# Attention, expert layer and cosine layer on one core: scores kept out of the output bank, loads and 64-bit conversions put in another order

## The chip, the cores and the metric

One of the eight cores of a Trainium2 chip runs the whole program. The metric is the time of one execution on the device, in microseconds (us); where several executions are told, the median stands for them.

## The reference

Three layers follow each other. Shapes: q, k, v are (4, 8, 576, 64); there are 2304 tokens of width 512.

```python
scores = scale * (q @ k.T)                       # per batch and head
mask   = (rel >= 0) & (rel < 128)                # rel = row - column
scores = where(mask, scores - slope[h] * abs(rel), -1e9)
attn   = softmax(scores);  x = (attn @ v) as (2304, 512)

P = exp(x @ w_gate - max)                        # (2304, 8)
8 times:  P /= rowsum(P);  P /= colsum(P);  P *= N / E
x2 = sum over 8 experts e of  P[:, e] * (relu(x @ w1[e]) @ w2[e])      # F = 1024

h = x2 @ w_in;  out = (h * cos(h)) @ w_out       # d_ff = 2048
```

`w_in` and `w_out` arrive as 64-bit floats, so the kernel sees each of their numbers as two 32-bit words and makes 32-bit floats of them itself.

## The kernel before, in words

**Engines and queues.** TensorE (PE) multiplies, VectorE (DVE), ScalarE (ACT) and GpSimd (POOL) work elementwise, and nearly every DMA is issued by SyncE (SP). The program's order of instructions is written out by hand: the order in which the Python emits them is the order on each engine, and an engine whose next instruction waits holds all that stand behind it. Tiles are tracked whole: an instruction that writes a tile waits for the earlier readers of that tile, also where it writes another part of it.

**Attention** goes head pair by head pair: `pi` = 0 to 15 (4 batches of 4 head pairs), five groups `u` of 128 query rows each (the last has 64), 80 groups in all. One turn `i` of the main loop (line 790) takes the pair of groups 2i and 2i+1 and does, in this order: scores of pair i (`emit_qk`), exponentials of pair i-1 (`emit_exp`, ACT), bias and row maximum of pair i (`emit_max`, DVE, L547), `gates`, the product with v of pair i-4 (`emit_AV`), transposes of the next head pair's q and k (`heads`, which calls `emit_T`), the copy of a finished head pair into `xr` (`emit_x`), transposes of the probabilities of pair i-3 (`emit_PT`), the scaling by the row sums of pair i-1 (`emit_norm`, POOL, L586), and two calls of `side`.

`emit_T(pi, piece)` turns a quarter of a head pair's q and k round: pieces 0 and 1 are the first and second part of q, 2 and 3 those of k. T(1,3) below means head pair 1, piece 3. The copies out of PSUM are made by DVE (qT, qL, the first part of kT) and ACT (the second part of kT, L511).

**PSUM in attention.** `ps_s` holds two banks for scores, `ps_t` three for transposes, `ps_g` one that gates and the pieces 0 and 2 share, and `xbank` is one tile of two banks in which the product with v is summed and in whose end the pieces 1 and 3 are put. The scores of pair 1 and pair 3 are put in the front of `xbank` and in a bank of `ps_t` (L525).

**Loads of q, k and v.** Each of the three has two buffers. At u = 1 and u = 3 of head pair `pi`, `heads` issues q and k of `pi + 2`; v of `pi + 2` is issued when `pi` is finished. Each is three DMAs on SP (lines 462 and 468).

**Gates.** 384 tokens make a half block, of which four become ready within attention. `gates` first transposes the last half's logits (`gate_block2`, a DVE copy at L381) and then, in the same turn, starts the next half (`gate_block`, an ACT copy); both use the one bank of `ps_g`. Two halves are ready at once only after the second batch.

**64-bit conversion.** `convert_f64` (L255) is a generator of ten steps; its caller takes one step at a time. Its tile `f` (called `raw`) has one buffer, so the next load (`load_f64`, L245 or L251, 512 KB in one or two DMAs) waits on SP until the words have been read. Before: DVE takes the exponent (L260, step 1), ACT scales it (L264, step 2), DVE joins sign and exponent (L267, step 4), masks the mantissa (L271, step 5), adds the low word (L275, step 6) and multiplies (L279, step 7); the next load is in step 8 and the store of the result (L287) in step 10. `side` takes two steps a turn, for four conversions between n = 8 and n = 47. The other 28 run in the expert layer's second and third token block (about 670 to 1420 us).

**Expert layer, token blocks 1 and 2.** Each step (32 a block) makes seven products in the order m = 5, 1, 4, 2, 3, 6, 7 (L966); after each comes one *couple* with a half of a second-layer product (`s_step`, L1105). A couple takes its 12 matmuls in about 2.08 us. Every second couple SP loads 512 KB of second-layer weights into one of four slots of `wbX` (L1133), for use three pairs of couples later; first-layer weights (`waX`, L115) are loaded almost two steps ahead. After the couple of m = 5, 1, 4, 2 and 7 there are two slots, after 3 and 6 one; each slot takes one step of the conversion. A conversion that starts with a step of the layer thus has its steps 5 and 6 after m = 4 and its steps 7 and 8 after m = 2. A step has seven couples, so in every other step the load into `wbX` comes with the couple of m = 2, and in the others with those of m = 4 and m = 3.

Of the kernel before, what the change touches and what calls it, by code (L numbers as in the profile page):

```python
# [18 lines left out]
P = 128  # L19
# [10 lines left out]
def tile_attention_moe_cos_ffn(ctx, tc, q, k, v, w_gate, w1, w2, w_in, w_out, out):  # L30
# [41 lines left out]
    with tc.manual_schedule():  # L72
# [164 lines left out]
        def load_f64(c):  # L237
            if c >= 4 * NU2:
                return
            s, x = divmod(c, 4)  # L240
            raw = u_pool.tile([P, 512, 2], I32, tag="u0", name=f"f64_{c}")
            if x < 2:
                for y in range(2):
                    kc = 2 * x + y
                    nc.sync.dma_start(  # L245
                        out=raw[:, y * FU:(y + 1) * FU, :].rearrange("p n t -> p (n t)"),
                        in_=w_in[kc * P:(kc + 1) * P, 2 * s * FU:2 * (s + 1) * FU],
                    )
            else:
                r0 = s * FU + (x - 2) * P  # L250
                nc.sync.dma_start(out=raw.rearrange("p n t -> p (n t)"), in_=w_out[r0:r0 + P, :])  # L251
            f64_t[c] = raw

        def convert_f64(c):
            raw = f64_t.pop(c)  # L255
            lo, hi = raw[:, :, 0], raw[:, :, 1]
            a = u_pool.tile([P, 512], I32, tag="u1", name=f"fa{c}")
            b = u_pool.tile([P, 512], I32, tag="u2", name=f"fb{c}")
            w = b.bitcast(F32)
            nc.vector.tensor_scalar(  # L260
                out=a, in0=hi, scalar1=20, scalar2=0x7FF, op0=ALU.logical_shift_right, op1=ALU.bitwise_and
            )
            yield
            nc.scalar.activation(out=a, in_=a, func=AF.Relu, scale=2.0 ** 23, bias=ebias)  # L264
            yield
            yield
            nc.vector.scalar_tensor_tensor(  # L267
                out=a, in0=hi, scalar=-2147483648, in1=a, op0=ALU.bitwise_and, op1=ALU.bitwise_or
            )
            yield  # L270
            nc.vector.tensor_scalar(  # L271
                out=b, in0=hi, scalar1=0xFFFFF, scalar2=0x100000, op0=ALU.bitwise_and, op1=ALU.bitwise_or
            )
            yield
            nc.vector.scalar_tensor_tensor(  # L275
                out=w, in0=lo.bitcast(U32), scalar=2.0 ** -32, in1=b, op0=ALU.mult, op1=ALU.add
            )
            yield
            nc.vector.scalar_tensor_tensor(  # L279
                out=w, in0=w, scalar=2.0 ** -20, in1=a.bitcast(F32), op0=ALU.mult, op1=ALU.mult  # L280
            )
            yield
            load_f64(c + 1)
            yield
            yield
            w32[c] = dram.tile([P, 512], F32, tag=f"w32_{c}", name=f"w32_{c}")
            nc.sync.dma_start(out=w32[c], in_=w)  # L287
# [89 lines left out]
        def gate_block2(j, lT, pool):  # L377
            ps = pool[0].tile([P, 512], F32, tag=pool[1], name=f"gateT{j}")
            for tt in range(GPB):
                nc.tensor.matmul(ps[:, tt * E:(tt + 1) * E], lT[:, tt * P:(tt + 1) * P], sel)  # L380
            nc.vector.tensor_copy(  # L381
                logits[:, j * GPB:(j + 1) * GPB, :].rearrange("p t e -> p (t e)"), ps[:, :GPB * E]
            )
# [138 lines left out]
        def emit_qk(n, pi, u):  # L522
            a = n % 2
            if n // 2 not in sbank:
                if n // 2 in (1, 3):  # L525
                    sbank[n // 2] = [xbank[:, :512], ps_t.tile([P, 512], F32, tag="t", name=f"s{n}_1")]
                else:
                    sbank[n // 2] = [ps_s.tile([P, 512], F32, tag="s", name=f"s{n}_{j}") for j in range(2)]
            grp[n] = sbank[n // 2] if a == 0 else sbank.pop(n // 2)
            c0, c1 = span(u)  # L530
            k0 = (u - 1) * P + c0
            for j in parts(u):
                o = grp[n][j][:, a * W2 + c0:a * W2 + c1]
                if u == NG - 1:
                    nc.tensor.matmul(o, qL[pi % 2], kT[pi][:, k0:k0 + c1 - c0])
                else:
                    nc.tensor.matmul(o, qT[pi % 2][hr[j], u * P:(u + 1) * P], kT[pi][hr[j], k0:k0 + c1 - c0])
# [126 lines left out]
        load_heads(0, k, kraw, "kr", nc.scalar, part=1)  # L664
        load_heads(1, q, qraw, "qr")
        load_heads(1, k, kraw, "kr")
        load_heads(0, v, vt, "v")
        make_identity(nc, ident)
        warm = ps_s.tile([P, 512], F32, tag="s", name="warm")

# [51 lines left out]
        distance(rel_li, rel_l, LW, hr)  # L722
        for t in qL:
            nc.gpsimd.memset(t, 0.0)
        load_heads(1, v, vt, "v")

        groups = [(pi, u) for pi in range(NP_ALL) for u in range(NG)]
        done_tok = 0
# [9 lines left out]
        def heads(n, pool=None):  # L738
            if n >= NGR:
                return  # L740
            pi, u = groups[n]
            if u < 4 and pi + 1 < NP_ALL:
                emit_T(pi + 1, u, pool)
                if u == 1:
                    load_heads(pi + 2, q, qraw, "qr")
                if u == 3:
                    load_heads(pi + 2, k, kraw, "kr")

        def side(n):
            nonlocal conv  # L750
            if n % 2 == 0 and n < 2 * NPAIR:
                set_last(n // 2)
            if n == 2:
                nc.sync.dma_start(out=wg_raw, in_=w_gate.rearrange("(k p) e -> p k e", p=P))
                nc.gpsimd.memset(wg, 0.0)
            if n == 3:
                load_f64(0)
            if 4 <= n < 8:
                load_raw((n - 4) // 2, "ab"[n % 2])
            if n == 8:  # L760
                nc.gpsimd.tensor_copy(wg[:, :, :E], wg_raw)
            if n == 12:
                conv += [prep_s(0), prep_a(0), prep_b(0), prep_s(1), prep_a(1), prep_b(1), prep_s(2)]
            if n == 48:
                early.append(stages(("moe", 0), xr[0]))
            if n == NGR:
                conv.append(prep_sb(0))
            if n == 56:
                early.append(combos(("moe", 0), xr[0]))
            if early and next(early[0], StopIteration) is StopIteration:  # L770
                early.pop(0)
            if 8 <= n < 50 and (chunk or n < 40):
                if not chunk:
                    chunk.append(convert_f64(n_f64[0]))
                    n_f64[0] += 1
                if next(chunk[0], StopIteration) is StopIteration:
                    chunk.pop(0)
            if n % 2 == 0 or 44 <= n < 56 or n >= 72:
                while conv and next(conv[0], StopIteration) is StopIteration:
                    conv.pop(0)  # L780

        def gates(n):
            nonlocal gate2, next_half
            for j, lT in gate2:
                gate_block2(j, lT, (ps_g, "g"))
            gate2 = []
            if n < NGR + 6 and next_half < 2 * NB and HB * (next_half + 1) <= done_tok:
                gate2.append((next_half, gate_block(next_half, (ps_g, "g"), ap_)))
                next_half += 1

# [3 lines left out]
        for i in range(NGR // 2 + 4):  # L794
            for g in pair(i):
                emit_qk(*g)
            for g in pair(i - 1):
                if g[0]:
                    emit_exp(*g)
            for g in pair(i):  # L800
                if g[0] != 1:
                    emit_max(*g)
            gates(2 * i - 2)
            if not i:
                emit_exp(*pair(0)[0])
                emit_T(0, 1, (ps_t, "t"))
                emit_T(0, 3, (ps_g, "g"))
                emit_max(*pair(0)[1])
            for g in pair(i - 4):
                emit_AV(*g)  # L810
            if i == 1:
                heads(0)
                heads(1)
                heads(2, (ps_t, "t"))
            elif i:
                if i == 2:
                    heads(3)
                heads(2 * i)
                heads(2 * i + 1)
            for n, pi, u in pair(i - 4):  # L820
                if u == NG - 1:
                    emit_x(pi)
                    load_heads(pi + 2, v, vt, "v")
                    if pi % NPAIR == NPAIR - 1:
                        done_tok += S
            for g in pair(i - 3):
                emit_PT(*g)
            if i < NGR // 2:
                emit_norm(pair(i - 1))
            else:  # L830
                for g in pair(i - 1):
                    emit_norm([g])
            for n in (2 * i, 2 * i + 1):
                side(n)
# [562 lines left out]
```

## Time and profile before

| | |
|---|---|
| three runs | 1983.06, 1985.64, 1985.77 us; median 1985.64 |
| the profiled execution | 1983.78 us, of which the span is 1982.0 us |
| PE busy | 1958.4 us (99%) |
| DVE, POOL, ACT busy | 79%, 49%, 44% |
| DMA | 540.05 MB, 272 GB/s on the mean, up to 343 GB/s in a fortieth of the span |
| chain that ended last | PE 88%, DVE 2%, DMA 1% |

The span runs from the first to the last instruction; the time is a little longer than it. A row of the timeline gives start and length in us, engine, line, operation and tiles, and in brackets how long the engine sat idle before and what ended that. Matmuls overlap in the pipe, so lengths of neighbours don't add up; what counts is when the next begins. In rows that list stretches, each engine has its busy time with its number of instructions in brackets, then come the granted clock of TensorE, the DMA engines' busy share and GB/s.

### The profile page before, as it was taken

How to read it: one execution, taken by the hardware profiler on the slowest of the kernel's cores; microseconds unless marked ns; L12 is line 12 of the kernel's file. 1: busy time of each engine (PE TensorE's matmuls, PEld its weight loads, DVE VectorE, ACT ScalarE, POOL GpSimd, SP SyncE). 2: the span in 40 equal slices, each digit the busy share in tenths (PEclk: the TensorE clock that was granted, in tenths of full speed). 3: DMA queues.
4: the chain of work that ended last, by engine and by line, in shares of the span. 5: the costliest groups of instructions: out<-in, count | busy, mean ns of one | idle time of the engine just before them, and what ended most of it. 6: DMA issues, size and time to landing. Idle time of an engine off the chain costs nothing.

```text
span 1982.0 us, 31160 instructions
## 1 busy us (share of the span) xinstructions
PE 1958.4 (99%) x10977; PEld 1823.2 (92%) x10977; DVE 1559.7 (79%) x2669; ACT 862.2 (44%) x1617; POOL 967.0 (49%) x939
## 2 busy tenths in 40 slices
PE   8999999999999999999999999999999999999999
PEld 6667899999999999999999999999999999998898
DVE  7885877777777788988988877888877776757766
ACT  6885444444444433333333433333233354554543
POOL 5673566666667545454536622545454523333221
PEclk9999999999999999999999999999999999999999
DMA  7854788888888999999999888999898765565552
GB/s 195 220 141 159 263 311 292 309 303 313 310 289 310 319 340 316 343 338 317 340 327 328 274 281 284 330 341 335 324 308 296 242 222 196 197 218 176 207 192 96
DMA packets 293755, 540.05 MB, mean 272 GB/s; under 512 B 80256, under 2 KB 141792, under 8 KB 286432
## 3 DMA queue, kind: packets, MB, share of 16 engines
q1 hardware_dynamic: 292240, 537.74, 78.6%
q8 instruction: 87, 1.43, 0.3%
q14 instruction: 68, 0.56, 0.1%
q10 hardware_dynamic: 1360, 0.33, 0.1%
HBM read 384.32 MB, written 153.67 MB: 271 GB/s over the span
## 4 chain that ended last, share of the span: by engine, by line
PE 88%; DVE 2%; DMA 1%; issue 0%; SPq 0%; POOL 0%; ACT 0%; ACTq 0%; DVEq 0%; POOLq 0%
PE gT L1105 23%; PE y_moe L966 19%; PE z_moe L966 10%; PE gT L1195 7%; PE gT L1196 7%; PE gT L1194 7%; PE y_ffn L966 5%; PE x_moe L966 5%; PE z_ffn L966 2%; PE x_ffn L966 1%; DMA wbX<-wdp 1%; SPq L96 0%; DVE waX L145 0%; DVE acc_ffn L1175 0%; DVE ta L939 0%
## 5 line engine op out<-in xcount | busy, mean ns | idle before, releaser
L1105 PE MATMUL gT<-hX,wbX 128*128 128x384 f32 x2688 | 538.3, 334 | 0.9 <-DMA wbX<-wdp 0.5
L1105 PEld LDWEIGHTS gT<-hX,wbX 128*128 128x128 f32 x2688 | 471.7, 188 | 3.5 <-DMA wbX<-wdp 1.5
L966 PE MATMUL y_moe<-xtT_moe,waX 128*128 128x384 f32 x1728 | 347.1, 335 | 0.6 <-ACT s_moe L995 0.6
L966 PEld LDWEIGHTS y_moe<-xtT_moe,waX 128*128 128x128 f32 x1728 | 304.3, 188 | 3.7 <-ACT s_moe L995 0.9
L1117 DVE TENSOR_TENSOR acc_moe<-gT,acc_moe 128x384 f32<-128x384 f32 x432 | 237.7, 550 | 77.7 <-PE gT L1105 76.0
L1196 PE MATMUL gT<-wbX,hX 128*128 128x512 f32 x660 | 258.0, 391 | 0.0
L1195 PE MATMUL gT<-wbX,hX 128*128 128x512 f32 x660 | 257.8, 391 | 0.0
L1194 PE MATMUL gT<-wbX,hX 128*128 128x512 f32 x660 | 257.7, 390 | 0.0
L995 ACT ACTIVATE s_moe<-y_moe 128x384 f32<-128x384 f32 x192 | 93.3, 486 | 345.6 <-PE y_moe L966 345.5
L1139 POOL TENSOR_TENSOR hodd<-hodd 128x384 f32<-128x384 f32 x128 | 155.4, 1233 | 139.4 <-DVE hX L1125 70.4
L1139 POOL TENSOR_TENSOR cX<-cX 128x384 f32<-128x384 f32 x128 | 146.6, 1165 | 153.6 <-DVE hX L1125 93.8
L955 POOL TENSOR_TENSOR hX<-cX,hX 128x768 fp32r<-128x768 f32 x44 | 83.5, 1914 | 249.3 <-ACT hX L952 208.6
L132 POOL TENSOR_TENSOR s<-ra 128x256 f32<-128x256 f32 x80 | 62.4, 780 | 251.3 <-DVE waX L145 178.9
L1185 DVE SCALAR_TENSOR_TENSOR acc_moe<-gT,prob,acc_moe 128x512 f32<-128x512 f32 x174 | 129.6, 747 | 37.6 <-PE gT L1196 35.8
L1196 PEld LDWEIGHTS gT<-wbX,hX 128*128 128x128 f32 x660 | 123.8, 188 | 26.0
L1194 PEld LDWEIGHTS gT<-wbX,hX 128*128 128x128 f32 x660 | 123.9, 188 | 25.4 <-DVE acc_ffn L1175 0.6
L1195 PEld LDWEIGHTS gT<-wbX,hX 128*128 128x128 f32 x660 | 123.9, 188 | 24.5
L911 ACT ACTIVATE hX<-cX 128x768 fp32r<-128x768 f32 x64 | 44.0, 687 | 218.7 <-DVE cX L998 218.7
L1125 DVE TENSOR_TENSOR hX<-cX,hX 128x768 fp32r<-128x768 f32 x112 | 132.4, 1182 | 1.1 <-ACT hX L1129 1.1
L1125 DVE TENSOR_TENSOR hX<-hodd,hX 128x768 fp32r<-128x768 f32 x112 | 127.5, 1138 | 0.9 <-ACT hX L1129 0.9
L966 PE MATMUL z_moe<-xtT_moe,waX 128*128 128x384 f32 x576 | 116.4, 335 | 0.4 <-DVE waX L145 0.2
L966 PE MATMUL z_moe<-xtB_moe,waX 128*128 128x384 f32 x576 | 115.9, 335 | 0.0
(210 smaller groups left out, 3771.9 us busy)
## 6 DMA issues: line engine op xcount, KB each, us to landing
waX<-wd SPq DMA_DIRECT2D x264, 512.0 KB, 5.5
wbX<-wdp SPq DMA_DIRECT2D x224, 512.0 KB, 6.5
wd<-waX SPq DMA_DIRECT2D x32, 1792.0 KB, 6.8
wdp<-sb SPq DMA_DIRECT2D x32, 1024.0 KB, 5.8
wdp<-wbX SPq DMA_DIRECT2D x96, 256.0 KB, 4.4
wbX<-wd SPq DMA_DIRECT2D x24, 1024.0 KB, 4.8
waX<-wd SPq DMA_DIRECT2D x88, 256.0 KB, 5.2
ra<-in_moe_w_dram SPq DMA_DIRECT2D x64, 256.0 KB, 7.4
```

Of the source, the lines that this page charges most:

```text
L132: nc.gpsimd.tensor_tensor(out=s4[:, o], in0=x, in1=y, op=op)
L955: eng.tensor_tensor(out=h[:, 1], in0=c, in1=h[:, 0].bitcast(F32), op=ALU.subtract)
L966: nc.tensor.matmul(ps[:, :HB], wa[:, WI[m], wl, kc, :], x[:, xl, kc, :], start=start and kc == 0 and n_ == 0, stop=stop and kc == 1 and n_ ...
L995: nc.scalar.activation(out=t["s", i], in_=ps[:, :HB], func=AF.Copy)
L1105: nc.tensor.matmul(ps[:, :HB], w[:, u, wl, d * P:(d + 1) * P], x[:, xl, u, :], start=m in (1, 5, 2) and n_ == 0, stop=m in (4, 3, 2) and n ...
L1117: nc.vector.tensor_tensor(out=a, in0=ps[:, :HB], in1=a, op=ALU.add)
L1125: nc.vector.tensor_tensor(out=x[:, 1], in0=H[:, q], in1=x[:, 0].bitcast(F32), op=ALU.subtract)
L1139: nc.gpsimd.tensor_tensor(out=H[:, t[0], c], in0=H[:, t[1], c], in1=H[:, t[2], c], op=ALU.subtract)
L1185: nc.vector.scalar_tensor_tensor(out=a, in0=ps, scalar=pe, in1=a, op0=ALU.mult, op1=ALU.add)
L1194: nc.tensor.matmul(ps, hf[f][:, 0, ts], wb[:, f, 0, :], start=f == 0, stop=False)
L1195: nc.tensor.matmul(ps, hf[f][:, 0, ts], wb[:, f, 1, :], start=False, stop=False)
L1196: nc.tensor.matmul(ps, hf[f][:, 1, ts], wb[:, f, 0, :], start=False, stop=f == 1)
```

## The change

It has four parts. First, the scores of pair 1 go to two banks of `ps_t` and those of pair 3 to `ps_s`; nothing but T pieces and the product with v uses `xbank`. In turn 3 the probabilities' transposes of pair 0 come before the T pieces instead of after them. Second, q and k are loaded five groups earlier (`pi + 3` where it was `pi + 2`, and those of head pair 2 in turn 0); v of head pair 0 is issued after q of head pair 2, and v of head pair 1 at n = 5. Third, `convert_f64` has another order of its ten steps, with the next load in step 6, and in attention it starts at n = 9, with its first load issued in turn 0. Fourth, a turn of `gates` either ends a half or begins one, never both.

```diff
@@ convert_f64
                 out=a, in0=hi, scalar1=20, scalar2=0x7FF, op0=ALU.logical_shift_right, op1=ALU.bitwise_and
             )
             yield
+            nc.vector.tensor_scalar(
+                out=b, in0=hi, scalar1=0xFFFFF, scalar2=0x100000, op0=ALU.bitwise_and, op1=ALU.bitwise_or
+            )
+            yield
             nc.scalar.activation(out=a, in_=a, func=AF.Relu, scale=2.0 ** 23, bias=ebias)
+            yield
+            nc.vector.scalar_tensor_tensor(
+                out=w, in0=lo.bitcast(U32), scalar=2.0 ** -32, in1=b, op0=ALU.mult, op1=ALU.add
+            )
             yield
             yield
             nc.vector.scalar_tensor_tensor(
                 out=a, in0=hi, scalar=-2147483648, in1=a, op0=ALU.bitwise_and, op1=ALU.bitwise_or
             )
-            yield
-            nc.vector.tensor_scalar(
-                out=b, in0=hi, scalar1=0xFFFFF, scalar2=0x100000, op0=ALU.bitwise_and, op1=ALU.bitwise_or
-            )
-            yield
-            nc.vector.scalar_tensor_tensor(
-                out=w, in0=lo.bitcast(U32), scalar=2.0 ** -32, in1=b, op0=ALU.mult, op1=ALU.add
-            )
+            load_f64(c + 1)
             yield
             nc.vector.scalar_tensor_tensor(
                 out=w, in0=w, scalar=2.0 ** -20, in1=a.bitcast(F32), op0=ALU.mult, op1=ALU.mult
             )
             yield
-            load_f64(c + 1)
             yield
             yield
@@ emit_qk
-                if n // 2 in (1, 3):
-                    sbank[n // 2] = [xbank[:, :512], ps_t.tile([P, 512], F32, tag="t", name=f"s{n}_1")]
-                else:
-                    sbank[n // 2] = [ps_s.tile([P, 512], F32, tag="s", name=f"s{n}_{j}") for j in range(2)]
+                pool, tag = (ps_t, "t") if n // 2 == 1 else (ps_s, "s")
+                sbank[n // 2] = [pool.tile([P, 512], F32, tag=tag, name=f"s{n}_{j}") for j in range(2)]
@@ before the loop
-        load_heads(0, v, vt, "v")
...
-        load_heads(1, v, vt, "v")
@@ heads
                 if u == 1:
-                    load_heads(pi + 2, q, qraw, "qr")
+                    load_heads(pi + 3, q, qraw, "qr")
                 if u == 3:
-                    load_heads(pi + 2, k, kraw, "kr")
+                    load_heads(pi + 3, k, kraw, "kr")
@@ side
-            if n == 3:
-                load_f64(0)
+            if n == 5:
+                load_heads(1, v, vt, "v")
...
-            if 8 <= n < 50 and (chunk or n < 40):
+            if 9 <= n < 50 and (chunk or n < 40):
@@ gates
-            for j, lT in gate2:
-                gate_block2(j, lT, (ps_g, "g"))
-            gate2 = []
-            if n < NGR + 6 and next_half < 2 * NB and HB * (next_half + 1) <= done_tok:
+            if gate2:
+                for j, lT in gate2:
+                    gate_block2(j, lT, (ps_g, "g"))
+                gate2 = []
+            elif n < NGR + 6 and next_half < 2 * NB and HB * (next_half + 1) <= done_tok:
@@ main loop
                 emit_T(0, 1, (ps_t, "t"))
                 emit_T(0, 3, (ps_g, "g"))
+                load_heads(2, q, qraw, "qr")
+                load_heads(0, v, vt, "v")
+                load_heads(2, k, kraw, "kr")
+                load_f64(0)
                 emit_max(*pair(0)[1])
+            if i == 3:
+                for g in pair(i - 3):
+                    emit_PT(*g)
             for g in pair(i - 4):
                 emit_AV(*g)
...
-            for g in pair(i - 3):
-                emit_PT(*g)
+            if i > 3:
+                for g in pair(i - 3):
+                    emit_PT(*g)
```

## Rows read from the trace of the kernel before

**Rows 1.** Stretches of the span: opening, rest of attention, conversions in the expert layer.

```profile
0.00:30.00 30.00, 23.62 (x155) 17.39 (x156) 20.42 (x117) 16.17 (x56) 12.36 (x37) 0.94 0.84 212
30.00:160.00 130.00, 122.65 (x1028) 83.47 (x1027) 100.61 (x430) 110.63 (x354) 91.41 (x156) 1.00 0.64 168
...
670.00:1420.00 750.00, 749.68 (x4318) 746.51 (x4318) 643.38 (x969) 266.95 (x466) 358.45 (x319) 1.00 0.91 323
```

**Rows 2.** Timeline of PE in the opening.

```profile
11.15 0.55 PE L494 MATMUL xbank<-ident,qr 128*128 128x128 f32 x3 [0.84 <-DVE anb L547]
...
13.19 0.65 PE L537 MATMUL s<-kT,qT 64*128 64x128 f32 x4 [0.94 <-DVE arr L579]
...
15.20 0.79 PE L537 MATMUL xbank<-kT,qT 64*128 64x256 f32 x1
...
18.43 0.55 PE L494 MATMUL xbank<-ident,qr 128*128 128x128 f32 x3 [1.33 <-DVE anb L547]
19.33 0.41 PE L494 MATMUL T<-ident,kr 128*128 128x128 f32 x2 [0.35 <-DMA kr<-in_k_dram]
...
20.33 0.70 PE L537 MATMUL s<-kT,qT 64*128 64x256 f32 x4
...
26.42 1.13 PE L537 MATMUL s<-kT,qT 64*128 64x256 f32 x8
...
29.01 0.41 PE L494 MATMUL T<-ident,kr 128*128 128x128 f32 x2 [0.72 <-DMA kr<-in_k_dram]
```

**Rows 3.** One microsecond of the opening as a stretch.

```profile
14.00:15.00 1.00, 1.00 (x5) 0.64 (x4) 0.59 (x6) 0.29 (x1) 1.00 (x3) 0.50 0.66 145
```

**Rows 4.** Timeline of DVE in the opening.

```profile
11.74 0.48 DVE L502 TENSOR_SCALAR qT<-xbank,inv 128x256 f32<-128x256 f32 x1 [0.30 <-PE xbank L494]
...
13.80 0.36 DVE L547 CUSTOM_DVE_ANT_0 sp<-s,biasl 128x192 f32<-128x192 f32 x1 [0.27 <-PE s L537]
...
17.25 0.42 DVE L547 CUSTOM_DVE_ANT_0 sp<-xbank,rel 128x256 f32<-128x256 f32 x1 [1.15 <-PE s L537]
...
21.70 0.43 DVE L547 CUSTOM_DVE_ANT_0 sp<-s,rel 128x256 f32<-128x256 f32 x1 [0.89 <-PE s L535]
```

**Rows 5.** Timeline of SP's queue: loads of q and k for head pair 2.

```profile
10.57 1.07 SPq L462 DMA_DIRECT2D qr<-in_q_dram  x2
...
14.40 0.93 SPq L462 DMA_DIRECT2D kr<-in_k_dram  x2
```

**Rows 6.** Timeline of PE at the gates of halves 1 and 2.

```profile
94.76 0.85 PE L371 MATMUL gate<-xr,wg 128*32 128x384 f32 x8 [0.72 <-DVE logits L381]
...
100.98 0.44 PE L494 MATMUL T<-ident,kr 128*128 128x128 f32 x2 [0.65 <-DVE logits L381]
```

**Rows 7.** Chain that ended last, where attention ends.

```profile
157.48 0.68 DVE xr L655
```

**Rows 8.** Waits of SP's queue, 670 to 1420 us: us in total, times, longest.

```profile
SPq L251 <- DVE fb L275: 41.8, 14, 4.5
```

**Rows 9.** Timeline of SP's queue around one conversion's load.

```profile
784.56 0.89 SPq L1133 DMA_DIRECT2D wbX<-wdp  x1
789.18 0.33 SPq L251 DMA_DIRECT2D f<-in_moe_w_out_dram  x1
```

**Rows 10.** Timeline of DVE in the same conversion.

```profile
783.76 0.69 DVE L267 SCALAR_TENSOR_TENSOR fa<-f,fa 128x512 int32<-128x512 int32 x1
...
786.78 1.23 DVE L271 TENSOR_SCALAR fb<-f 128x512 int32<-128x512 int32 x1
```

**Rows 11.** Timeline of PE: first use of the weights issued at 784.56.

```profile
796.49 1.20 PE L1105 MATMUL gT<-hX,wbX 128*128 128x384 f32 x6
```

**Rows 12.** Line 1133 at 784.56 alone: issue to landing.

```profile
DMA to landing us min/median/max: 9.9/9.9/9.9
```

**Rows 13.** Line 1133 at 1372.59 alone: issue to landing.

```profile
DMA to landing us min/median/max: 9.3/9.3/9.3
```

**Rows 14.** Line 1133, all 179 issues from 670 to 1420 us: issue to landing.

```profile
DMA to landing us min/median/max: 3.8/6.8/12.7
```

## The prediction

> **What bounds the kernel now.** I read the stretches first, to find where PE is short of work at all. From 670 to 1420 us, where most conversions run, PE is busy 749.7 of 750 us; in the opening it is busy 23.6 of 30, and in the rest of attention 122.7 of 130 [rows 1]. So a change can win only in attention, and behind it it can only lose. Then I went through PE's timeline in the opening, looking at the bracket of each row: 0.84, 0.94, 1.33, 0.35 and 0.72 us of idle time, ended by DVE three times and by a landing k twice [rows 2]. The third view is the granted clock: at 14 to 15 us it is 0.50, the lower level of 1.2 GHz, after a stretch in which PE idled 0.84 and 0.94 us [rows 2, 3]. DVE's own timeline tells whether it would be late without PE: it idles 0.30, 0.27, 1.15 and 0.89 us, each time for PE [rows 4]. The two hold each other up; neither is full. Last come SP's waits, because loads are moved past them [rows 5, 8, 9].
>
> **Scores out of the output bank.** In turn 1, T(1,1) writes `xbank` and waits until DVE has read the scores of pair 1 there: PE idles 0.84 us before 11.15 [rows 2]. In `ps_t` this wait is gone. What is late next is DVE: its copies of T(1,1) and T(1,2) begin at 11.74 after idling 0.30 [rows 4], so the scores of turn 2, which need those copies, come only 0.30 us sooner: 12.9 for 13.19 [rows 2]. Of 0.84 I take 0.30.
>
> Turn 3 gives more. The scores of pair 3 need the end of T(2,0), the copy of kT and the banks of pair 2, which DVE reads from 13.80 (now 13.5) for 0.8 us. With T(1,3) and T(2,0) taking about 0.5 us each at the full clock (three transposes took 0.55 at 18.43 [rows 2]) and the copy behind them 0.48 (such a one at 11.74 [rows 4]), I put them at 14.5; before, they began at 15.20 [rows 2]. Their eight matmuls take 1.13 us at the full clock (those at 26.42 [rows 2]); at the clock granted here they ran until DVE could start at 17.25 [rows 4]. So DVE starts at 15.7. Three of its four maxima took 1.2 us, from 17.25 [rows 4] to 18.43, where PE was released [rows 2]; four take 1.5, to 17.2. PE meanwhile makes the probabilities' transposes of pair 0 (which the change puts here; they lie between T(2,2) at 19.33 and 20.33, so under 1.0 us, and I take 0.75) and T(2,1) without the 1.33 us for `xbank` [rows 2], then T(2,2): 15.6 + 0.75 + 0.4 + 0.25 = 17.0. The scores of pair 4 need the banks of pair 3, free at 17.2, where before they began at 20.33 [rows 2]: **3.1 us sooner**. This holds if DVE follows. Its copies, sums and bias behind the maxima took from 18.75 to 20.81, where its idle time before 21.70 begins [rows 4], 2.1 us with some waiting in it; from 17.2 that is 19.3 for the next maxima, 2.4 us sooner. I take 2.8 for the two together. If the clock falls nevertheless, the eight matmuls cost 0.8 us more (1.9 from 15.20 to the end, for 1.13), T(1,3), T(2,0) and the half pair of scores before them another 0.6: 1.4 us are left. Ends: 1.0 and 3.8.
>
> **Loads of q and k.** k of head pair 2 is issued at 14.40 [rows 5] and awaited at 19.33 [rows 2], 4.9 us later. q of head pair 2 stood behind two loads of v, six DMAs of 0.53 us each (1.07 for two [rows 5]), and can go at 10.57 - 3.2, about 7.5 to 8, once T(0,1) has been read; k follows behind q and v of head pair 0 at about 11. With 4.9 us each lands by 13 and 16, ahead of T(2,0) at 13.9 and T(2,2) at 16.7: the 0.35 goes (it is in the 2.8), and so does the 0.72 at 29.01 [rows 2], where k of head pair 3 now has five groups more. DVE is busy around that place, so I take 0.6 of 0.72. A wait is added: SP now holds the load for head pair pi + 3 until T(pi + 1) has left the buffer. Behind it stand raw weights, v and stores; v is needed two and a half turns later (a turn takes 3 us: the scores at 20.33 and 26.42 are two apart), so I cost this at nothing; if the cover is gone, it costs one transfer's 4.9 us once.
>
> **Gates.** The one double turn costs 0.72 us at 94.76; a turn later a T piece waits 0.65 for the same bank [rows 6]. With the halves apart the 0.72 goes; the T pieces of the next two turns may wait for ACT's and DVE's copies instead, 0 to 0.65 each. I take a gain of 0.5, with ends of 1.4 and 0.
>
> What is won in attention is passed on: the chain leaves attention through the last copy into `xr` at 157.48 [rows 7], and what follows is issued behind it. Sum for attention: 2.8 + 0.6 + 0.5 = 3.9, ends 1.0 and 5.5.
>
> **The conversions.** Nothing is added: the same five DVE instructions, one ACT instruction and the same DMAs. In attention each takes the same ten steps one step later. The load is moved from step 8 to step 6, but it doesn't go out earlier. At 789.18 SP had already been waiting at it, for the instruction of step 6 [rows 9]; such waits come to 41.8 us over 14 loads of w_out alone [rows 8]. Now it waits for another instruction of the same step 6, the joining of sign and exponent, 0.69 us [rows 10]. What changes is the queue: what SP issued between the two places now stands behind that wait. That is a load of `waX`, needed two steps later, and in every other step a load into `wbX`. By the list of SP's issues 11 of the 28 conversions lie so.
>
> One of them: the weights are issued at 784.56, land 9.9 us later at 794.5 and are used at 796.49: 2.0 us to spare [rows 9, 11, 12]. After the change DVE reaches step 6 where it began masking, at 786.78, and needs 0.69 us [rows 10], so the load goes at 787.6 and the weights, behind two issues of 0.35 us, at 788.3: 3.8 us later, 1.8 too late if they take 9.9 us again, and in time with the 6.8 us of the median [rows 14]. Landings of over 8 us come at four of the eleven (the first this one, the last at 1372.59 with 9.3 us [rows 13]); the other seven have 5 us or more to spare, or are not delayed. So the loss lies between 0 and some 6 us (four times about 1.5). If they took long because much was queued ahead of them, they join that queue later now and lose less; I take 1.2. Against it stands that ACT waits less for the exponent, worth up to 0.5 us; I leave it in the range.
>
> Here one rule of the Trainium skill speaks against the change. The page DMA: Bandwidth & Descriptors (Anatomy of one DMA) says that the engines moving data never wait on a semaphore: the waiting is done by the issuing sequencer, before dispatch. The row at 789.18 agrees: 4.6 us after 784.56, with nothing issued between. By the rule every load behind the moved one is held; without it the loss would be 0 and the sum 1.2 us lower.
>
> **The sum.** 3.9 - 1.2 = 2.7 us off the profiled execution's 1983.8 us (a span of 1982.0 and 1.8 around it), which gives 1981.1. That execution is 1.9 us under the median of the three runs, 1985.64; against the median I forecast **1982.9 us**.
>
> **Rivals.** *A: SP's hold costs more than attention wins (slower).* If DVE is as late for step 6 as it was before, the load goes at 789.18 as now, the weights at 789.9 and, at 9.9 us, 3.3 us late [rows 9, 11, 12]. Four such, with smaller ones at the other seven (about 5 us later, against 5 to 7 us to spare), come to 12 us: 1985.6 - 3.9 + 12 = 1993.7. It decides from a hold of 5 us with landings of 8 us and more. For it: DMA is busy 0.91 of that stretch [rows 1]. Against: the median landing leaves 5 us. With landings halfway, 6 us, the result is 1987.7.
> *B: the opening's gain turns into another wait (no change).* DVE and ACT have to follow PE, and PE's next scores now wait for the maxima of the pair just before, in the same two banks. If the clock falls as before, 1.4 is left, and with the later parts failing and the hold at 1.2 the result is 1985.4. For it: the 0.84 us in turn 1 is already mostly lost to DVE. Against: DVE's 2.6 us of idle time [rows 4].
> The Trainium skill, TensorE: Matmul & The Clock Gate (The HAM clock gate), says that the gate's rhythm isn't tied to a kernel's start. By that the low clock at 14 us may come in one execution and not in the next, and gains here would differ from run to run; one trace can't show it.
> *C: all of it works (more).* 5.5 in attention and no hold: 1980.1.
>
> **How the numbers follow.** About 0.2% or 4 us is what a measurement of this kernel can tell from no change, so faster begins under 1981.7. Chances: the forecast 0.45, B 0.22, C 0.18, A 0.15. The forecast's own range is 1980.5 to 1985, A's reaches from 1987 up with most of it past 1989.6; with C below, B and the milder part of A above, 8 in 10 lie between 1978.5 and 1988.5. Faster: C and somewhat under half of the forecast, 0.38. Slower by over 4 us: A without its mildest part, 0.12. The same: 0.50.
>
> **What would show it.** Right: no idle time of PE before T(1,1) and T(2,1); the scores of pair 4 at about 17 us and a clock of 1.00 up to 20; no wait for k at 26; no double turn of gates; in the conversions, loads into `wbX` issued right behind the load of `f` and PE waits on `wbX` of 0 to 2 us in sum. Wrong: PE waits on `wbX` of 5 us or more (A); scores of pair 4 at 19 or later (B); or attention's end less than 2 us sooner than before although the scores of pair 4 come at 17, with the difference given back in waits of PE for DVE or ACT further on.

## The result: slower by 0.9%

The changed kernel takes 2002.34 us (median of 6 runs, 1999.5 to 2007.13) beside 1985.7 for the kernel before (6 runs, 1983.06 to 1989.35): a ratio of 1.0086, with a 95% interval of 1.0073 to 1.0099. Forecast were 1982.9 us and a range of 1978.5 to 1988.5. The profiled execution of after took 2006.46 us (span 2004.7), 4 us above its own median; its parts below therefore add up to 22.7 us against the 1983.8 of before, where the medians differ by 16.6.

The same stretches as in [rows 1], after (busy us of PE, weight loads, DVE, ACT, POOL with their instructions; granted clock; DMA share; GB/s):

```profile
0.00:30.00 30.00, 26.27 (x189) 19.88 (x189) 22.48 (x129) 20.48 (x69) 14.77 (x42) 1.00 0.81 204
30.00:160.00 130.00, 117.28 (x952) 80.11 (x948) 96.72 (x415) 103.93 (x336) 84.71 (x145) 0.97 0.63 165
670.00:1420.00 750.00, 739.03 (x4222) 732.75 (x4221) 625.33 (x942) 261.72 (x453) 345.74 (x312) 1.00 0.89 316
```

PE makes 34 matmuls more than before in the opening and 76 fewer in the rest of attention; in the expert layer it loses 10.65 us of busy time. The chain that ended last has the last copy into `xr` at 164.33 (first row), where [rows 7] had 157.48, so attention ends 6.85 us later instead of 3.9 sooner. In the page's chain by line the landings of second-layer weights (`DMA wbX<-wdp`) now take 4% of the span, where they took 1% before (second row). The page's group of the second-layer products has 11.0 us of waiting for them (third row), where before it had 0.5 (last row).

```profile
164.33 0.68 DVE xr L653
```
```profile
PE gT L1110 20%; PE y_moe L971 18%; PE z_moe L971 9%; PE gT L1201 7%; PE gT L1200 7%; PE gT L1199 7%; PE y_ffn L971 5%; PE x_moe L971 4%; DMA wbX<-wdp 4%; PE z_ffn L971 2%; PE x_ffn L971 1%; DVE hX L1130 1%; DMA ra<-w 1%; DVE acc_moe L1122 1%; DVE cX L1018 0%
...
L1110 PE MATMUL gT<-hX,wbX 128*128 128x384 f32 x2688 | 540.8, 336 | 11.4 <-DMA wbX<-wdp 11.0
```
```profile
L1105 PE MATMUL gT<-hX,wbX 128*128 128x384 f32 x2688 | 538.3, 334 | 0.9 <-DMA wbX<-wdp 0.5 <-DVE acc_moe L1117 0.2
```

**The opening went as forecast.** PE's timeline, against [rows 2]:

```profile
13.02 0.49 PE L535 MATMUL s<-kT,qT 64*128 64x128 f32 x4 [1.62 <-ACT sp L560]
...
14.14 1.34 PE L535 MATMUL s<-kT,qT 64*128 64x256 f32 x8
...
16.76 0.76 PE L535 MATMUL s<-kT,qT 64*128 64x256 f32 x4
```

The scores of pair 4 begin at 16.76, 3.57 us sooner. In turn 1 little of that is won: PE's two waits of 0.84 and 0.94 us have become one of 1.62, ended by ACT and not by DVE, and the scores of turn 2 come 0.17 us sooner, not 0.30. No piece of T waits for `xbank`, and the clock at 14 to 15, where [rows 3] had 0.50, is 1.00:

```profile
14.00:15.00 1.00, 1.00 (x9) 0.83 (x8) 0.97 (x8) 0.97 (x4) 1.00 (x4) 1.00 0.86 202
```

**Then attention gives it back, and more.** PE's timeline of after, and below it DVE's, whose second and third rows stand behind PE's last two stalls (in the bracket: idle us before, and what ended it). The last row, of POOL, belongs to the long DVE row above it:

```profile
32.99 0.41 PE L494 MATMUL T<-ident,kr 128*128 128x128 f32 x2 [1.05 <-DMA kr<-in_k_dram]
...
36.51 0.96 PE L637 MATMUL xbank<-ptT,v 128*64 128x256 f32 x4 [1.31 <-DVE anb L545]
...
47.34 0.59 PE L533 MATMUL s<-kT,qL 128*128 128x192 f32 x2 [2.13 <-DVE anb L545]
...
83.86 1.47 PE L535 MATMUL s<-kT,qT 64*128 64x256 f32 x8 [2.41 <-DVE anb L545]
```
```profile
39.94 0.43 DVE L260 TENSOR_SCALAR fa<-f 128x512 int32<-128x512 int32 x1 [2.94 <-DMA f<-in_moe_w_in_dram]
...
45.83 0.43 DVE L264 TENSOR_SCALAR fb<-f 128x512 int32<-128x512 int32 x1 [2.60 <-DMA w<-fb]
...
80.78 2.27 DVE L260 TENSOR_SCALAR fa<-f 128x512 int32<-128x512 int32 x1 [2.38 <-DMA f<-in_moe_w_out_dram]
```
```profile
80.41 2.35 POOL L161 TENSOR_TENSOR wbX<-rb,wbX 128x1024 fp32r<-128x1024 f32 x1
```

DVE stands three times for the conversion: twice for raw words that have not landed, and at 45.83 for the store of the conversion before, whose tile `fb` it wants to write. The trace of before has no such wait of DVE from 0 to 165 us. The third wait costs twice: it moves DVE's operation to a time at which POOL is at work, and there it takes 2.27 us instead of 0.41 (more on this at the end). The two long stalls of PE are followed by half clock, as are two in the expert layer:

```profile
48.00:51.00 3.00, 2.98 (x14) 1.62 (x15) 1.58 (x9) 1.05 (x5) 1.89 (x4) 0.50 0.54 120
85.60:88.60 3.00, 3.00 (x21) 2.76 (x21) 2.93 (x16) 0.55 (x3) 1.55 (x4) 0.50 0.19 43
864.00:867.00 3.00, 3.00 (x10) 3.00 (x11) 0.79 (x2) 1.15 (x2) 3.00 (x5) 0.50 1.03 408
1342.00:1345.00 3.00, 3.00 (x11) 3.00 (x11) 1.89 (x3) 0.77 (x2) 0.00 (x0) 0.50 1.05 413
```

**The expert layer.** SP's waits from 670 to 1420 us, against [rows 8] (the loads of w_in, L245, had 25.6 us there, 10 times, 3.8 the longest), then SP's timeline at the conversion of [rows 9] (everything lies 7.8 us later here: PE's group of matmuls at 784.97 in before begins at 792.76):

```profile
SPq L251 <- DVE fa L275: 61.6, 13, 6.3
...
SPq L245 <- DVE fa L275: 47.7, 12, 6.0
```
```profile
787.50 1.54 SPq L1138 DMA_DIRECT2D wbX<-wdp  x1
789.35 0.51 SPq L216 DMA_DIRECT2D wd<-hla  x1
790.62 0.37 SPq L115 DMA_DIRECT2D waX<-wd  x1
796.85 0.33 SPq L251 DMA_DIRECT2D f<-in_moe_w_out_dram  x1
797.28 0.60 SPq L115 DMA_DIRECT2D waX<-wd  x1
797.93 0.43 SPq L1138 DMA_DIRECT2D wbX<-wdp  x1
```

SP issues nothing from 790.99 to 796.85, and the weights that went out ahead of the raw words in [rows 9] go out behind them, 5.6 us later by the shifted clock (797.93 - 784.56 - 7.8). DVE's step 6 and PE's first use of these weights:

```profile
796.14 0.68 DVE L275 SCALAR_TENSOR_TENSOR fa<-f,fa 128x512 int32<-128x512 int32 x1
```
```profile
801.07 1.31 PE L1110 MATMUL gT<-hX,wbX 128*128 128x384 f32 x6 [0.86 <-DMA wbX<-wdp]
...
806.25 1.28 PE L1110 MATMUL gT<-hX,wbX 128*128 128x384 f32 x6 [0.74 <-DMA wbX<-wdp]
```

The dearest of the eleven waits, with the half clock behind it (groups of six matmuls that take 1.21 us take 2.29 and 1.77):

```profile
860.28 1.21 PE L971 MATMUL y_moe<-xtT_moe,waX 128*128 128x384 f32 x6
863.88 2.29 PE L1110 MATMUL gT<-hX,wbX 128*128 128x384 f32 x6 [2.39 <-DMA wbX<-wdp]
865.97 1.77 PE L971 MATMUL z_moe<-xtT_moe,waX 128*128 128x384 f32 x6
867.57 1.21 PE L1110 MATMUL gT<-hX,wbX 128*128 128x384 f32 x6
```

### The profile page after: what moved, and what is told of

Its sections match the earlier page's. It is cut to its first block, busy times and chain, and to the rows that moved or that the text cites. A ratio compares the mean times of both kernels' runs of the same rounds, so it can differ in the third digit from the quotient of the medians.

```text
span 2004.7 us, 31145 instructions
## 1 busy us (share of the span) xinstructions
PE 1966.8 (98%) x10977; PEld 1829.1 (91%) x10977; DVE 1556.8 (78%) x2669; ACT 865.5 (43%) x1617; POOL 962.2 (48%) x939
## 4 chain that ended last, share of the span: by engine, by line
PE 82%; DMA 4%; DVE 4%; issue 1%; ACT 0%; POOL 0%; SPq 0%; ACTq 0%; DVEq 0%; POOLq 0%
PE gT L1110 20%; PE y_moe L971 18%; PE z_moe L971 9%; PE gT L1201 7%; PE gT L1200 7%; PE gT L1199 7%; PE y_ffn L971 5%; PE x_moe L971 4%; DMA wbX<-wdp 4%; PE z_ffn L971 2%; PE x_ffn L971 1%; DVE hX L1130 1%; DMA ra<-w 1%; DVE acc_moe L1122 1%; DVE cX L1018 0%
## 5 line engine op out<-in xcount | busy, mean ns | idle before, releaser
L1110 PE MATMUL gT<-hX,wbX 128*128 128x384 f32 x2688 | 540.8, 336 | 11.4 <-DMA wbX<-wdp 11.0
```

The costliest lines, as they stand in the source:

```text
L1110: nc.tensor.matmul(ps[:, :HB], w[:, u, wl, d * P:(d + 1) * P], x[:, xl, u, :], start=m in (1, 5, 2) and n_ == 0, stop=m in (4, 3, 2) and n ...
```

## The experiments

Each kernel ran in 5 rounds beside the kernel before, whose medians there are 1984.82 to 1985.81 us. Below, the products with `wbX` are those of the second layer in token blocks 1 and 2 (`gT<-hX,wbX`). Everything between the end of attention and the first of them takes 525.3 to 526.3 us in all traces, and everything from the start of the last group of six on 369.0 to 369.1. So each profiled time splits into two stretches, read from PE's timeline: the start of the first gate product of the last half (attention's end), and the stretch from the start of the first to the start of the last group of these products ("layer"). "Idle" is PE's idle time up to attention's end, "half clock" the us granted at 0.50 up to there. These four columns are each from one profiled execution.

| kernel | attention's end | idle | half clock | layer | median | ratio to before, 95% |
|---|---|---|---|---|---|---|
| before | 158.20 | 13.7 | 3.4 | 929.4 | 1985.7 | |
| after | 165.05 | 17.6 | 6.8 | 945.2 | 2002.34 | 1.0086 [1.0073, 1.0099] |
| e1_conv_only | 163.89 | 16.4 | 10.2 | 938.1 | 2000.11 | 1.0078 [1.0065, 1.0090] |
| e2_old_conv | 169.37 | 19.1 | 13.7 | 929.7 | 1995.19 | 1.0050 [1.0038, 1.0062] |
| e3_late_load | 167.97 | 18.7 | 13.7 | 928.0 | 1992.72 | 1.0040 [1.0028, 1.0052] |
| e4_early_qk | 160.76 | 16.4 | 3.4 | 931.6 | 1987.67 | 1.0006 [0.9995, 1.0016] |
| e5_open_only | 157.78 | 14.9 | 0 | 931.6 | 1985.57 | 0.9997 [0.9989, 1.0006] |
| e6_split_load | 164.11 | 15.2 | 10.2 | 929.0 | 1988.11 | 1.0014 [1.0005, 1.0023] |
| e7_load6_old | 157.85 | 13.8 | 3.4 | 938.9 | 1996.08 | 1.0058 [1.0046, 1.0071] |
| e8_open_split | 157.87 | 13.9 | 3.4 | 929.2 | 1983.95 | 0.9997 [0.9988, 1.0006] |
| e9_new_late | 163.11 | 17.1 | 6.8 | 927.4 | 1987.71 | 1.0015 [1.0006, 1.0024] |
| e10_old_early | 162.19 | 16.4 | 3.4 | 929.4 | 1989.32 | 1.0019 [1.0011, 1.0028] |
| e11_old_early_gap | 163.22 | 15.2 | 10.2 | 930.4 | 1988.23 | 1.0014 [1.0005, 1.0023] |
| e12_part_early | 157.09 | 14.8 | 0 | 929.9 | 1984.54 | 0.9995 [0.9986, 1.0004] |

### e1_conv_only and e2_old_conv: the conversion alone, and all but it

e1 is the kernel before with the new `convert_f64`; e2 is the changed kernel with the old one.

> The kernel before with the new order of the ten conversion steps alone. Theory H (the load in step 6 holds SP's queue, so weights for wbX come late): some 12 to 14 us are lost between 670 and 1420 us, as in the whole change, and little in attention: 1997 to 2001 us. Rival W (the masking now writes its tile right behind the DMA that stores the last result, so DVE waits for that store): the same total, but with DVE waits on the store of 2 to 3 us each in attention too: 2000 to 2004. Rival Q (the loss in attention comes from the earlier q and k loads): attention ends within 1 us of before here, the total is 1997 to 2000.

> The whole change, but with the conversion steps in their old order. H and W: no wait of PE on wbX over 1 us in sum, and attention keeps the opening's 3 us or so: 1981 to 1984 us. Q: attention still ends 5 us or more later than before, because k and the conversion's words are held behind q and k loads: 1989 to 1993.

e1 has nearly the whole loss, 15.3 us on its own kernel before (1984.82). Its time fits H and W alike. Q fails, because attention ends 5.7 us late without the earlier loads. In its attention DVE has one long wait, for the store that I had not counted, and PE stands behind it:

```profile
78.21 1.92 DVE L264 TENSOR_SCALAR fb<-f 128x512 int32<-128x512 int32 x1 [2.38 <-DMA w<-fb]
```
```profile
80.95 2.03 PE L537 MATMUL s<-kT,qT 64*128 64x256 f32 x8 [2.94 <-DVE anb L547]
```

e2's layer is back at 929.7, but its attention is the slowest of all. DVE's waits from 0 to 165 us (us in total, times, longest):

```profile
DVE fa L260 <- DMA f<-in_moe_w_out_dram: 8.0, 2, 5.4
DVE fa L260 <- DMA f<-in_moe_w_in_dram: 6.2, 1, 6.2
```

Its time lies 2 us above the range of Q and refutes H and W. So with q and k loaded early the raw words come too late for DVE. The load in step 6 helps there: e10 below differs from e2 in that alone, in attention only, and its attention ends 7.2 us sooner.

### e3_late_load and e7_load6_old: the place of the load alone

```diff
@@ e3: after, load back in step 8
-            load_f64(c + 1)
             yield
...
+            load_f64(c + 1)
@@ e7: before, load in step 6 behind the low word's addition
+            load_f64(c + 1)
             yield
...
-            load_f64(c + 1)
```

> The whole change, but the next load of the conversion is put back two steps (behind the last multiplication, step 8); the new order of the arithmetic stays. H: PE's waits on wbX go back to under 2 us and the time to 1988 to 1991 (what attention loses stays). W: the conversions stay late because DVE still waits for the store, and more than half of the loss between 670 and 1420 us is left: 1996 to 2002.

> The kernel before with the next load moved from step 8 to step 6, right behind the instruction that reads the words last; the arithmetic keeps its old order. H: PE waits on wbX of 6 us or more, 1992 to 2000 us, with attention's end within 1.5 us of before. W: 1984 to 1987.

The two agree; e7's time lies in H's range, e3's 1.7 us above it. With the load in step 8 the layer is at 928.0 although the arithmetic is in the new order; with the load in step 6 it is at 938.9 although the arithmetic is old and nothing else is changed. e7's attention is as before, so its 10 us are those of the load's place in the expert layer alone. SP's waits and the group of the products in e7, then the same in e3:

```profile
SPq L251 <- DVE fb L275: 70.3, 14, 7.1
...
SPq L245 <- DVE fb L275: 47.9, 12, 5.5
```
```profile
L1105 PE MATMUL gT<-hX,wbX 128*128 128x384 f32 x2688 | 539.4, 335 | 8.5 <-DMA wbX<-wdp 8.2 <-DVE acc_moe L1117 0.2
```
```profile
SPq L251 <- DVE fa L275: 32.9, 14, 3.7
...
SPq L245 <- DVE fa L275: 25.6, 11, 3.9
```
```profile
L1110 PE MATMUL gT<-hX,wbX 128*128 128x384 f32 x2688 | 537.7, 334 | 0.3 <-DMA wbX<-wdp 0.2
```

### e4_early_qk and e5_open_only: loads alone, opening alone

> The kernel before with only the loads moved: q and k five groups sooner, v of the first two head pairs later. Q: SP stands at waits for transposes and the later loads come late, attention ends 4 to 8 us later: 1990 to 1994 us. H and W: 1984 to 1986, the two waits for a landing k gone and nothing else.

> The kernel before with only the scores' banks and the probabilities' transposes of turn 3 changed. Theory F (in attention DVE stands still for a conversion's words that land after it asks for them, and attention that runs ahead asks sooner): the opening wins 3 us or more by 20 us, and DVE waits of 1 to 3 us for the words of f take part of it back: 1982 to 1986 us. Rival R (the waits of PE for DVE's maxima at 35 to 90 us come from putting all scores into the same two banks): the same waits of PE, but no DVE wait for a DMA: 1987 us or more.

Neither can be told from no change. e4's time lies between the two ranges named. e5's lies in the range of F, but the waits of DVE for raw words that F rests on did not come (0.2 us in all). e5 has the banks and the order of the transposes without the earlier loads, and its gain in turn 3 turns at once into waits of PE for k and q (PE's timeline of e5):

```profile
18.34 0.41 PE L494 MATMUL T<-ident,kr 128*128 128x128 f32 x2 [1.43 <-DMA kr<-in_k_dram]
...
24.67 0.41 PE L494 MATMUL T<-ident,qr 128*128 128x128 f32 x2 [0.96 <-DMA qr<-in_q_dram]
```

e4 has the loads without the banks; DVE waits 2.46 us for raw words at 76.01, and attention ends 2.6 us later.

### e6_split_load and e8_open_split: the load in step 6 only in attention

```diff
+            if c < 3:
+                load_f64(c + 1)
             yield
...
+            if c >= 3:
+                load_f64(c + 1)
```

e6 is the changed kernel with this; e8 has also the old order of arithmetic and the old q and k loads.

> The whole change, but the next load is in step 6 only for the conversions in attention and back in step 8 for those of the expert layer. Theory H (the position of the load decides between 670 and 1420 us): waits of PE on wbX under 2 us, attention's end as in the whole change, 5 to 7 us late: 1988 to 1992 us. Rival W (the arithmetic's order matters there): 1996 or more.

> The kernel before with the scores' banks, the transposes of turn 3 and the gates changed, the old order of the arithmetic, and the load in step 6 in attention alone. F: the words land earlier there, DVE's waits for them stay under 2 us and 2 to 4 us are won: 1981 to 1984 us. R: 1986 us or more.

e6 takes 14 us off the changed kernel's median; its layer is 929.0. What is left of the loss is attention's. e8's time lies in F's range, and DVE's waits for raw words stay at 0.5 us, but its attention ends only 0.3 us sooner and it can't be told from no change: PE waits 0.85 and 2.39 us for q and k at 14.52 and 19.52, with half clock behind the second.

### e9_new_late, e10_old_early, e11_old_early_gap: the rest of the square

> The kernel of e8 (banks, order of PT, gates; load in step 6 for the attention's conversions and in step 8 for the expert layer's) with the new order of the conversion's arithmetic, and with the q and k loads where they were before. With e8 (old order, loads as before; attention ends at 157.87, 1983.95 us) and e6 (new order, early loads; 164.11, 1988.11 us) it is the third corner of a square. If the new order alone costs the attention its 6 us, because step 2 writes the tile that step 10 of the conversion before is still storing (as in e1, 163.89), it ends at 163 to 165 and takes 1989 to 1991 us, with a wait of DVE for the store of 2 to 3 us in 0 to 165. If the early q and k loads cost it, it ends near 158 and takes 1984 us.

> e6 with the old order of the conversion's arithmetic: the fourth corner (old order, early loads, load in step 6 in the attention and step 8 in the expert layer). If only the new order costs, the attention keeps the opening's 3 us and ends at 154.5 to 156: 1980 to 1982 us, with no wait of DVE for raw words over 1 us. If the early loads cost by themselves, because SP's queue then issues the raw words behind them and DVE, which comes sooner, waits for them, there are waits for f of 4 to 9 us in all, the attention ends at 160 to 165, and the time is 1986 to 1991 us.

> e10 with two empty turns between the conversions of the attention (they start in turns 9, 21, 33 and 45 in place of 9, 19, 29 and 39), so that a load has two turns (some 3.3 us) more to land. If what the attention gives back is DVE standing still for words that have not landed, those waits go (under 1 us in all), the opening's gain is kept to the end of the attention (154.5 to 156.5), and the time is 1980 to 1982.5 us. If the loss comes from the crowded queue itself (q, k and v landing late for TensorE), the waits on f go and the attention still ends at 159 or later: 1985 us or more.

With the opening, the gates and the split load in all four, attention ends at 157.87 (old order, loads as before), 163.11 (new order), 162.19 (early loads) and 164.11 (both). Either part alone costs 4 to 5 us and both 6.2: the costs don't add. e9 ends attention as the first branch said and takes 1.3 us less than it said (its layer is 1.8 us shorter than e8's); e10 went as its second branch said. e9's row is the wait for the store again, e10's are the waits for words:

```profile
78.31 1.88 DVE L264 TENSOR_SCALAR fb<-f 128x512 int32<-128x512 int32 x1 [2.34 <-DMA w<-fb]
```
```profile
DVE fa L260 <- DMA f<-in_moe_w_out_dram: 3.6, 1, 3.6
DVE fa L260 <- DMA f<-in_moe_w_in_dram: 2.6, 1, 2.6
```

In e11 the turns named are values of `n`, two to a turn of the main loop. It refutes the simple form of my theory and agrees in its numbers with the rival set beside it, the crowded queue itself. All of DVE's waits for words are gone, and attention still ends at 163.22: PE now waits for v, as the rival has it, and longer still for POOL, which the rival doesn't explain, with half clock behind both (PE's timeline of e11):

```profile
36.37 0.40 PE L640 MATMUL xbank<-ptT,v 128*64 128x256 f32 x1 [2.28 <-DMA v<-in_v_dram]
...
111.89 0.48 PE L604 MATMUL pt<-ident,sp 128*128 128x128 f32 x1 [3.64 <-POOL sp L587]
```

### e12_part_early: only the opening's share of the early loads

```diff
                 if u == 1:
-                    load_heads(pi + 2, q, qraw, "qr")
+                    if pi:
+                        load_heads(pi + 2, q, qraw, "qr")
@@ turn 0
+                load_heads(0, v, vt, "v")
+                load_heads(2, q, qraw, "qr")
+                load_heads(2, k, kraw, "kr")
```

> e8 (banks, order of PT, gates, old order of the arithmetic, load in step 6 only in the attention) with only the opening's share of the early loads: the first two v loads move behind the transposes of turn 0, the q and k of head pair 2 come right behind them, and from head pair 3 on the q and k loads stay where they were before, so SP's queue has no head pair more in front of the raw words and of v. If the attention gives the gain back because the queue runs one head pair ahead, the waits of e8 for q and k of 0.8 and 2.4 us in 14 to 20 go, no wait of DVE for f and of TensorE for v over 1 us comes in 30 to 90, the attention ends at 154.5 to 156, and the time is 1980 to 1982 us. If any change of that order brings a stall of TensorE of over 2 us somewhere, with half clock behind it, the attention ends at 158 to 163 and the time is 1984 to 1989 us.

The stalls at 14 to 20 are gone and none comes in 30 to 90, but the q of head pair 2 now costs one of 3.43 us at 24.89:

```profile
24.89 0.30 PE L497 MATMUL T<-ident,qr 128*128 128x128 f32 x1 [3.43 <-DMA qr<-in_q_dram]
```

Attention ends at 157.09, 1.1 us sooner than before, and the time is level with before. In the code the v of head pair 1 stands behind this q and k, at n = 5, not before them. Neither expectation was met: a stall of over 2 us came, but without half clock behind it. No version ran measurably faster than the kernel before.

## Why the prediction was wrong

**The opening: right in size, wrong in what becomes of it.** The term of 2.8 us was 3.57 at the scores of pair 4, and the clock stayed at 1.00. But "What is won in attention is passed on" failed. Only the traces with the new banks and all early loads (after, e2, e3, e6, e10, e11) have PE busy 15.0 of the 15 us from 15 to 30 (e5: 11.7), and in each of them it stalls behind that: for k, for v, for POOL, or for a DVE that waits for raw words. The prediction named this way of failing (attention's end not sooner though the scores of pair 4 are) without giving it a price for words or v. Its sum for attention has a slip that decides nothing: the upper ends 3.8 and 1.4 with the 0.6 make 5.8, not 5.5.

**The earlier loads: "I cost this at nothing".** This term failed. One head pair more stands in SP's queue ahead of v and of the raw words. v is late in e10 and e11 (PE waits 2.30 us at 37.29 and 2.28 at 36.37), raw words in e10 (6.2 us), and e10 against e8 (which differ in these loads, their order in turn 0 and the start of the conversions) puts it at 4.3 us of attention. The price that the prediction named for lost cover, one transfer's 4.9 us, is of that size, but it was in neither the sum nor its ends.

**The conversion in attention: "Nothing is added".** A wait was added. Masking the mantissa moved from step 5 to step 2, so it writes `fb` right behind the store of the conversion before (step 10), and `fb` has one buffer. That took 2.60, 2.38 and 2.34 us in after, e1 and e9, and e9 against e8 puts the new order at 5.2 us of attention. In e1 and e9 the wait also pushes DVE's operation into one of POOL's, where it takes 1.92 and 1.88 us instead of 0.41.

**Half clock.** I thought of it only as something that the opening might lose. After six of the seven stalls of PE of over 2.1 us in the rows above the clock fell to 0.50 within 2 us; e12's is the seventh. Over all traces it is sixteen of twenty such stalls; besides e12's, those without half clock are 2.39 us before 82.47 in e10, 2.58 before 856.64 in e4 and 2.26 before 856.62 in e7. At 863.88 the stall of 2.39 us is followed by two groups of matmuls whose starts are 2.09 and 1.60 us apart instead of 1.04: 1.6 us more. In attention the 6.85 us of after split into 3.8 of idle time, 1.7 of half clock (3.4 us more of it, at half speed) and 1.3 that I can't assign.

**The load's hold: the term of 1.2 us, bounds 0 to 6.** This is the largest error: 15.8 us in the profiled execution, 8.7 in that of e1, whose layer has the same code, 10.3 by e7's median (1996.08 to 1985.81) and 14.2 by e6's against after's. The mechanism, and three of the four landings named, were right. DVE reached step 6 at 796.14, that is 788.3 by the clock of before instead of 786.78, and SP's load went at 796.85, 1.4 us later than forecast. Of the four weights foreseen, behind the raw words by two issues, three cost PE 0.74, 0.82 and 0.78 us, and the one issued at 903.52 in before landed in time. Of "the other seven" one, issued at 1257.93 in before with 1.0 us to spare, cost 0.17. All eleven loads that change places together cost 2.5 us, well inside the bounds.

The step that failed is the one from "11 of the 28 conversions lie so" to "the loss lies between 0 and some 6 us": only loads that change places with the raw load were counted. The other 8.5 us of waiting fall on loads that keep their place. PE waits longest for weights that are issued ten to thirteen issues after a raw load, not behind it: 2.39 us at 863.88 (issued at 852.46, landed 11.4 us later), 2.18 at 1340.68 (11.8), 1.17 at 741.67 (12.6), 0.86 at 801.07 (13.5). These already had under 2 us to spare before, one of them 0.04. With the longer hold more landings are slow: of the first 190 loads into `wbX`, 70 took over 8 us in after, 75 in e7 and 77 in e1, the three with the load in step 6 in the layer, and 41 to 56 in the other eleven traces (47 in before, 41 in e3). That the place of the load does this is shown; that it's the many issues right behind the hold which slow each other is argued. I had held landings at the values of before. PE's idle time in the layer grew from 0.9 to 11.4 us, two of the waits bring half clock that costs some 1.6 us each, and about 2 us I can't assign.

The rule that I weighed, the Trainium skill's DMA: Bandwidth & Descriptors (Anatomy of one DMA), that the issuing sequencer does the waiting, held: nothing was issued from 790.99 to 796.85. What the release does to landings does not follow from it.

**Rival A** was this mechanism, priced at 12 us, with the chance of 0.15. It was closer than the forecast, but its arithmetic (four late weights of 3.3 us) was not what happened. **Rival B**, a gain in the opening that turns into another wait, is what e5 and e12 show by themselves, though not by B's mechanism: they wait for q and k, not for the maxima of the pair before.

**The gates** can't be read apart: the double turn and its 0.72 us are gone in e8, but e8 has half clock in the opening that e5 has not. In e8 a T piece waits 0.79 us at 100.01 for ACT's copy.

What stays open: why four of the twenty stalls had no half clock behind them, what makes the layer of after 7 us longer than e1's with the same code, and which part of after varies by 7 us from run to run.

## What to carry to other kernels

When a load is moved ahead on an in-order queue, don't only shift the transfers that it passes: list every consumer with little to spare, also those far behind: here the longer hold went with 70 to 77 slow landings instead of 41 to 56, and TensorE's longest waits were for loads issued ten to thirteen issues behind the one that held the queue. When steps of a pipelined routine are put in another order, check each tile's first write against the last reader of the round before, its store included. A gain on an engine that three others feed lasts only as far as the next transfer; price the first wait behind it before booking the gain.

## What was not expected of the hardware

The DVE operations on 128x512 that take the exponent or mask the mantissa take 0.41 and 0.42 us in the median of before. They took 2.27 us at 80.78 in after, 1.92 at 78.21 in e1 and 1.88 at 78.31 in e9, each right behind a wait of over 2 us for a DMA. The wait isn't what slowed them: at 39.94 and 45.83 in after they took 0.43 behind waits of 2.94 and 2.60. In all three a POOL operation of 2.35 us (L161) was already under way (in after from 80.41 to 82.76), and DVE's ended 0.3 us after it. Over all traces 102 operations of this kind took more than 1 us; every one began while POOL was at work and ended 0.25 to 0.33 us after that POOL operation. The 1.23 us in [rows 10] is one of them. Why the one holds the other no run here takes apart, and not every POOL operation does: at 59.81 in after DVE took 0.42 beside POOL's scaling by the row sums.

One issue on SP, usually 0.32 to 0.5 us, took 1.54 us at 787.50 above.
